# Two decode layers on one core: twelve partitions for a quarter MB of the last w2, other cuts of w1, and an earlier hand-over between two PSUM banks

## The chip, the cores and the metric

The kernel runs on one core of a Trainium2 chip. The metric is the device time of one execution in microseconds, the median of several runs. Everything is float32 and the batch is 8 rows of one token each, so the kernel reads far more than it computes with: 368.46 MB of weights and caches go from the chip's memory into the core's on-chip memory in each execution.

## What is computed

Two layers, each an attention block and then a dense block, with the same weights both times:

```python
x = x + attn(layernorm(x))       # q = x @ wq [1024 x 4096]; 32 heads of 128, 4 kv heads, 4096 cached keys
x = x + mlp(layernorm(x))        # gelu(x @ w1 [1024 x 3584] + b1) @ w2 [3584 x 1024] + b2
x = x + attn(layernorm(x))
x = x + mlp(layernorm(x))
```

`attn` takes the softmax of the scores over all cached keys and ends with `wo` [4096 x 1024].

## The kernel before, in words

All loads go into one large buffer, `arena` (L59), 128 partitions with 218 units of 1 KB in each. One unit of all partitions is 128 KB. `take` and `give` (L68, L72) mark units as used and free. All loads stand in one list, `stream`, in the order of their use (L526 to L545). `pump` (L178) is called at each `give`: as long as the first load of the list finds its units free, it is issued from the SyncE queue (SP) as one DMA over all 128 partitions. At run time SP then waits, load by load, until the engines that last read or wrote those units have finished with them.

Weights and caches lie on the partitions so that each matmul has 32 columns of weights (the batch, padded) and up to 512 columns of data. Four such matmuls, for four groups of 32 columns of TensorE, can run side by side; each writes its own 32 partitions of a PSUM bank. I call such a group a strip. A float32 matmul of the program is two matmul records in the trace, called passes here (a transpose is one).

The stages of a layer are `expand("q")` (L192), the attention over 8 batch rows (L460), `project("o")` (L288), `expand("i")` for w1 and `project("p")` for w2.

- `expand` works in two units of output columns, for w1 1792 columns each. For each unit it goes through the 8 blocks of 128 input rows (kt), at L209. After a unit its result is scaled by VectorE (DVE, L234, L237), and `hidden_unit` (L272) is put off until a later `flush`: it transposes the unit with matmuls (L246), adds b1 and computes gelu on DVE and ScalarE (ACT).
- `project` goes through the 28 blocks of 128 hidden columns (kt), each four units of w2 wide. In layer 1 the first `pairs` = 25 blocks go by 512 columns into a second PSUM bank `y2` (L327), even blocks into strips 0 and 1, odd ones into 2 and 3. Then ACT copies that bank to `scratch` (`fold`, L310) and four matmuls add the copy into the first bank `y` (`add_fold`, L313, whose matmuls have the line L295 of the helper `into`). The blocks 25 to 27 go by 256 columns straight into `y`. Half way, at block 14, `add_bias` (L298) adds b2: DVE makes four diagonals (L302), one matmul takes them into `y2` (L307), DVE makes four more in the same buffer, a second matmul takes those; then x itself is added (L350).
- The end of the kernel is the last `project`, an ACT copy of `y` into `x_row` (L358) and the output DMA (L637).

In layer 0 the weights go through a ring of four slots of 1 MB (L518). In layer 1 they are loaded in large pieces: w1 as two pieces of 56 units (L544), w2 as seven pieces of 40, 28, 20, 12, 6, 4 and 2 units (L545). I call these seven pieces w2.0 to w2.6.

In the attention, the maximum of each row of scores is spread over the partitions by a diagonal, which DVE makes (L396), and a matmul with ones (L400).

Of the kernel before, what the change touches and what calls it, by code (L numbers as in the profile page):

```python
# [39 lines left out]
AT_QZ, AT_ROW, AT_S, AT_ROW2 = 200, 208, 212, 203  # L40
AT_H = 200
Q_AT = (0, 48, 72, 32)
# [5 lines left out]
@with_exitstack  # L48
def decode_layers(ctx: ExitStack, tc: tile.TileContext, x, kc, vc, wq, wo, w1, w2, out):

# [43 lines left out]
    row_x = scratch  # L94
    r_at, dg_at, nb_at, dl_at, rl_at = 0, 2 * DH, 3 * DH, 3 * DH + HQ, 3 * DH + 2 * HQ

# [11 lines left out]

    def open_last():
        take(AT_H, 6, "last")  # L110
        nc.gpsimd.memset(place(AT_H, 5), 0.0)
        nc.vector.tensor_reduce(sel_f.rearrange("p (h m) -> p h m", h=2), ident.rearrange("p (e h m) -> p h m e", e=2, h=2), AX.X, ALU.add)
        nc.vector.tensor_scalar(nmean4.rearrange("p (j m) -> p j m", j=4), sel_x.unsqueeze(1).to_broadcast([P, 4, HQ]), -1.0 / D, None, op0=ALU.mult)
# [77 lines left out]

    def expand(name, unit, rs, finish, hooks={}, tail=(), hold=0):  # L192
        heights = [(unit // P - j + 3) // 4 * P for j in range(4)]
        for u in range(2):
            acc = big_ps()
# [76 lines left out]
    def hidden_unit(u, wide=False):  # L272
        nt = NFT // 2
        t0 = u * nt
# [12 lines left out]

    def project(name, n_k, lhs, rsum, hooks={}, bias=None, halves=False, pairs=0):  # L288
        y = big_ps()
# [25 lines left out]

        w = 32 if rsum is None else B
        g = 0
        for i, base, n_kb in loads(name):
            for c in range(n_kb):
# [3 lines left out]
                if kt < pairs:  # L323
                    if q % 2 == 0:
                        assert c + 1 < n_kb
                        j = kt % 2 * 2 + q // 2
                        nc.tensor.matmul(y2[32 * j:32 * j + 32, :], mine, arena[:, e:e + CH], start=(kt < 2), stop=(kt >= pairs - 2))  # L327
                else:
                    cut = [(q, 0, Q4)] if kt < n_k - 1 or not halves else [(2 * (q % 2) + i, q // 2 * P, P) for i in range(2)]
                    for j, a, n in cut:  # L330
                        into(j, a, n, mine, arena[:, e:e + n], stop=(kt == n_k - 1 and a + n == Q4 and (not pairs or bias is not None)))
                        e += n
                g += 1
                if c + 1 == n_kb:
# [39 lines left out]
    def scores(key, spare=False, late=False):  # L374
# [10 lines left out]
        if j == HKV - 1:  # L385
# [108 lines left out]
    def weights(name, dram, parts, kept=0):  # L494

        for u in range(dram.shape[0]):
            a = 0
            end = dram.shape[2] - (kept if u == 1 else 0)
            for i, (at, n) in enumerate(parts[u]):
                cols = min(n * KB, end - a)  # L500
                stream.append((((name, u) if dram.shape[0] > 1 else name, i), at, n, dram[u, :, a:a + cols]))
                a += cols
# [112 lines left out]
    for layer in range(2):  # L615
        pieces.update({key: at for (e, key), at in places.items() if e == layer})
        rs = layernorm(x_row, rsum)
        if layer == 0:
            expand("q0", W, rs, query_unit, {(1, "end"): keep}, hold=6)
            flush()  # L620
            last = attention(range(B), kept, after={6: park, 7: set_aside})
            set_aside_rest()
        else:
            expand("q1", W, rs, query_unit_late, {(0, 4): clear, (0, "end"): put_back_rest, (1, 3): put_back, (1, 6): open_queries_late}
                   | {(1, i): (lambda key=key: early(key)) for i, key in zip((1, 2, 4, 5), first)}, tail=(moves[1], stays))
# [6 lines left out]
        rs = layernorm(x_row, rsum, whole=layer == 1)  # L632
        expand(f"i{layer}", F // 2, rs, lambda u: hidden_unit(u, wide=layer == 1))
# [6 lines left out]
_INS = ['A_x', 'A_k_cache', 'A_v_cache', 'A_wq', 'A_wo', 'B_w1', 'B_w2']  # L640

# [17 lines left out]
def _down(w):  # L659
    return w.reshape(1, -1, P, D).transpose(0, 2, 1, 3).reshape(1, P, -1)  # L660


def _down_halves(w):
    import numpy as _np
    r = _np.array(_down(w))
    t = r[:, :, -D:].reshape(1, P, 4, 2, P)
    r[:, :, -D:] = t.transpose(0, 1, 3, 2, 4).reshape(1, P, D)
    return r


def _across(w):
    return w.reshape(NT, P, 2, -1).transpose(2, 1, 0, 3).reshape(2, P, -1)

# [4 lines left out]
    'A_v_cache': lambda a: a.reshape(B, HKV, P, -1).transpose(0, 2, 1, 3).reshape(B, P, -1),  # L678
    'A_wq': _across,
    'B_w1': _across,  # L680
    'A_wo': _down,
    'B_w2': _down_halves,
}

# [22 lines left out]
```

## Time and profile before

| | us |
|---|---|
| median of 3 runs (870.35 to 871.34) | 871.21 |
| the profiled execution, its own time | 870.82 |
| its span in the profile | 869.0 |
| PE, DVE, ACT busy in the span | 537.0, 180.3, 52.9 |

The profiled execution is 0.39 us below the median; 1.82 us of its time lie outside the span. Times in the views count from the start of the span. "DMA share" is the mean busy share of the core's 16 DMA engines, and a share a little over 1.00 comes from transfers that overlap in the records. PEclk is the granted clock of TensorE as a part of 2.4 GHz. In the timeline, a row is a run of instructions of one line, with its start, its length and their number; in brackets stands the idle time of the engine before it and what ended it.

### The profile page before, as it was taken

How to read it: one execution, taken by the hardware profiler on the slowest of the kernel's cores; microseconds unless marked ns; L12 is line 12 of the kernel's file. 1: busy time of each engine (PE TensorE's matmuls, PEld its weight loads, DVE VectorE, ACT ScalarE, POOL GpSimd, SP SyncE). 2: the span in 40 equal slices, each digit the busy share in tenths (PEclk: the TensorE clock that was granted, in tenths of full speed). 3: DMA queues.
4: the chain of work that ended last, by engine and by line, in shares of the span. 5: the costliest groups of instructions: out<-in, count | busy, mean ns of one | idle time of the engine just before them, and what ended most of it. 6: DMA issues, size and time to landing. Idle time of an engine off the chain costs nothing.

```text
span 869.0 us, 8920 instructions
## 1 busy us (share of the span) xinstructions
PE 537.0 (62%) x3932; PEld 179.6 (21%) x3932; DVE 180.3 (21%) x603; ACT 52.9 (6%) x84; POOL 3.5 (0%) x14
## 2 busy tenths in 40 slices
PE   0456574655657576866576777777564655655566
PEld 0112121211212122222232122222121211211222
DVE  0001231313122232200110033332231313120011
ACT  0100000000000011000000010000000000000100
POOL 0000000000000000000000000000000000000000
PEclk9877787777777788768977798977787777777889
DMA  9999999999999999999999999999999999999997
GB/s 393 434 435 435 429 432 432 434 432 432 434 429 432 434 419 428 412 416 418 421 420 417 408 425 438 434 434 432 432 435 431 435 434 435 432 431 436 426 422 295
DMA packets 17078, 369.06 MB, mean 425 GB/s; under 512 B 1904, under 2 KB 2064, under 8 KB 3728
## 3 DMA queue, kind: packets, MB, share of 16 engines
q1 hardware_dynamic: 16896, 368.35, 99.2%
q8 instruction: 30, 0.49, 0.2%
q10 hardware_dynamic: 144, 0.15, 0.1%
q14 instruction: 8, 0.07, 0.0%
HBM read 368.46 MB, written 0.03 MB: 424 GB/s over the span
## 4 chain that ended last, share of the span: by engine, by line
DMA 74%; PE 22%; DVE 2%; ACT 1%; issue 0%; SPq 0%; ACTq 0%; DVEq 0%
DMA arena<-in_A_k_cache_dram 26%; DMA arena<-in_A_v_cache_dram 22%; DMA arena<-in_B_w_dram 15%; DMA arena<-in_A_wq_dram 8%; PE sps L440 7%; PE sps L383 6%; DMA arena<-in_A_wo_dram 4%; PE sps L209 3%; PE sps L295 2%; PE sps L327 1%; PE sps L455 1%; PE sps L418 1%; PE sps L246 0%; ACT arena L407 0%; DVE arena L391 0%
## 5 line engine op out<-in xcount | busy, mean ns | idle before, releaser
L383 PE MATMUL sps<-arena 128*32 128x512 f32 x992 | 144.2, 720 | 119.5 <-DMA arena<-in_A_k_cache_dram 107.4
L440 PE MATMUL sps<-arena 128*32 128x512 f32 x1024 | 149.2, 722 | 9.0 <-DMA arena<-in_A_v_cache_dram 8.9
L209 PE MATMUL sps<-arena,xnT 128*32 128x512 f32 (+3 forms) x656 | 77.8, 580 | 50.4 <-DMA arena<-in_B_w_dram 26.5
L383 PEld LDWEIGHTS sps<-arena 128*32 128x32 f32 x992 | 31.5, 125 | 197.1 <-DMA arena<-in_A_k_cache_dram 99.5
L448 DVE SCALAR_TENSOR_TENSOR scratch<-sps,misc,scratch 128x128 f32<-128x128 f32 x192 | 67.4, 351 | 6.8
L295 PE MATMUL sps<-arena,oT 128*32 128x256 f32 (+1 forms) x504 | 46.3, 503 | 25.5 <-DMA arena<-in_B_w_dram 12.4
L418 PE MATMUL sps<-ident,arena 128*128 128x128 f32 x128 | 30.5, 382 | 43.5 <-ACT arena L407 31.6
L440 PEld LDWEIGHTS sps<-arena 128*32 128x32 f32 x1024 | 32.7, 129 | 83.0 <-issue 70.9
L391 DVE TENSOR_SCALAR_CACHE_REDUCE arena<-sps 128x512 f32<-128x512 f32 x32 | 22.1, 691 | 126.8 <-PE sps L383 126.8
L407 ACT ACTIVATE arena<-arena,bias 128x1024 f32<-128x1024 f32 x16 | 18.4, 1147 | 493.4 <-DVE scratch L404 493.4
L457 DVE TENSOR_TENSOR oT<-sps,scratch 128x8 f32<-128x8 f32 x64 | 11.1, 173 | 156.9 <-PE sps L455 156.9
L209 PEld LDWEIGHTS sps<-arena,xnT 128*32 128x32 f32 x656 | 22.1, 122 | 94.4 <-DMA arena<-in_A_wq_dram 36.1
L455 PEld LDWEIGHTS sps<-misc,scratch 128*128 128x128 f32 x128 | 21.7, 213 | 66.2 <-DVE scratch L448 40.9
L446 DVE TENSOR_SCALAR scratch<-sps,misc 128x128 f32<-128x128 f32 x64 | 22.0, 344 | 53.0 <-PE sps L440 53.0
L418 PEld LDWEIGHTS sps<-ident,arena 128*128 128x128 f32 x128 | 19.4, 188 | 52.1 <-ACT arena L407 35.3
L327 PE MATMUL sps<-arena,oT 128*32 128x512 f32 x120 | 17.6, 744 | 17.9 <-DMA arena<-in_A_wo_dram 17.9
L455 PE MATMUL sps<-misc,scratch 128*128 128x8 f32 x128 | 27.6, 288 | 1.3 <-DVE scratch L448 1.3
L295 PEld LDWEIGHTS sps<-arena,oT 128*32 128x32 f32 x504 | 17.2, 136 | 52.4 <-DMA arena<-in_A_wo_dram 19.8
L400 PE MATMUL sps<-scratch,misc 128*128 128x128 f32 x32 | 7.8, 326 | 19.1 <-DVE scratch L396 18.8
L423 DVE COPY arena<-sps 128x512 f32<-128x512 f32 x16 | 11.1, 692 | 38.9 <-PE sps L418 38.9
L327 PE MATMUL sps<-arena 128*32 128x512 f32 x100 | 14.4, 669 | 5.7 <-DMA arena<-in_B_w_dram 5.7
L425 PE MATMUL sps<-scratch,misc 128*128 128x32 f32 x32 | 10.0, 404 | 12.5 <-DVE arena L423 12.5
(99 smaller groups left out, 160.4 us busy)
## 6 DMA issues: line engine op xcount, KB each, us to landing
arena<-in_B_w_dram SPq DMA_DIRECT2D x26, 1024.0 KB, 8.5
arena<-in_A_wo_dram SPq DMA_DIRECT2D x15, 1024.0 KB, 8.3
arena<-in_B_w_dram SPq DMA_DIRECT2D x2, 7168.0 KB, 45.0
arena<-in_A_wq_dram SPq DMA_DIRECT2D x13, 1024.0 KB, 8.1
arena<-in_A_k_cache_dram SPq DMA_DIRECT2D x3, 4096.0 KB, 18.3
arena<-in_A_v_cache_dram SPq DMA_DIRECT2D x3, 4096.0 KB, 24.5
arena<-in_A_v_cache_dram SPq DMA_DIRECT2D x4, 2048.0 KB, 12.0
arena<-in_B_w_dram SPq DMA_DIRECT2D x1, 5120.0 KB, 39.8
```

Of the source, the lines that this page charges most:

```text
L209: nc.tensor.matmul(acc[32 * j:32 * j + 32, r * P:(r + len(ts)) * P], xnT[:, kt * B:kt * B + 32], blocks[:, ts[0] - t0:ts[-1] - t0 + 1:4], ...
L295: nc.tensor.matmul(y[32 * j:32 * j + 32, a:a + n], weights, data, start=(j not in begun), stop=stop)
L327: nc.tensor.matmul(y2[32 * j:32 * j + 32, :], mine, arena[:, e:e + CH], start=(kt < 2), stop=(kt >= pairs - 2))
L383: nc.tensor.matmul(ps[32 * g:32 * g + 32, :], q[:, c:c + 32], kt[:, g * CH:(g + 1) * CH], start=(j == 0), stop=(j == HKV - 1))
L391: nc.vector.tensor_scalar(row[:, half * CH:(half + 1) * CH], ps, SCALE, None, op0=ALU.mult, op1=ALU.max, accum_out=st["mx"][:, half:half + 1])
L407: nc.scalar.activation(row, row, AF.Exp, bias=bias, scale=1.0, accum_out=ls)
L418: nc.tensor.transpose(pp[:, t * P:(t + 1) * P], row[:, c:c + P], ident)
L423: nc.vector.tensor_copy(s[:, half], src)
L440: nc.tensor.matmul(o[32 * g:32 * g + 32, :], s[:, g], v[:, g * CH:(g + 1) * CH], start=(half == 0), stop=(half == NH - 1))
L446: nc.vector.tensor_scalar(r, o[:, 0:P], sel_t[:, 0:1], None, op0=ALU.mult)
L448: nc.vector.scalar_tensor_tensor(r, o[:, t * P:(t + 1) * P], sel_t[:, t:t + 1], r, op0=ALU.mult, op1=ALU.add)
L455: nc.tensor.matmul(po[:, 0:REP], scratch[:, a:a + DH], sel_h, start=True, stop=True)
```

## The change

Three things, each in a few lines of the diff.

1. **w2 of layer 1.** The first 512 columns of the first w2 block (128 rows of 2 KB, 256 KB) are no longer part of w2.0 to w2.6, whose sizes become 40, 28, 18, 12, 6, 4, 2 units. These 128 rows are laid out again, on 12 partitions in 11 groups (the last has 8 rows, padded to 12): 12 rows of 22 KB, 264 KB. Four DMAs load them, each with three rows: partitions m, m+4, m+8 for m = 0 to 3. They stand in the stream after w1 and ahead of w2.0. So that matmuls can use them, the weights of that block are cut into the same 11 groups: 11 small matmuls with the identity and two DVE copies (`low_weights`) at the start of the last `project`. After block 8, 11 matmuls over 12 partitions (`low_products`) add the groups into `y2`, into strips 0 and 2 in turn. The hidden values' buffer moves from unit 200 to 212 to make room.
2. **w1 in 2048 and 1536 columns** instead of twice 1792, in both layers. In layer 1 the two pieces are then 64 and 48 units.
3. **22 blocks in the second bank** instead of 25: `fold` comes after block 21, and the blocks 22 to 27 go straight into `y`.

Besides, the diagonal of the attention's maximum goes: one transpose (a single pass) of the broadcast maximum takes the place of L396 and L400. In layer 0, the last w2 block is taken by four matmuls in place of eight.

```diff
+FU = (2048, 1536)
-AT_H = 200
+AT_H = 212
+AT_LOW, AT_LH = 184, 206
+LOW = 12
+NLOW = (P + LOW - 1) // LOW
...
             take(at, n, key)
-            nc.sync.dma_start(out=arena[:, at * KB:at * KB + src.shape[1]], in_=src)
+            dst = arena[:, at * KB:at * KB + src.shape[1]]
+            if key[0] == "low":
+                dst = arena[key[1]:LOW:4, AT_LOW * KB:AT_LOW * KB + src.shape[1]]
+            nc.sync.dma_start(out=dst, in_=src)
...
+        def low_weights():
+            pt = small_ps("pt")
+            for s in range(NLOW):
+                n = min(LOW, P - s * LOW)
+                nc.tensor.matmul(pt[0:n, s * 32:(s + 1) * 32], ident[:, s * LOW:s * LOW + n], lhs[:, 0:32], start=True, stop=True)
+            for a, b, n in ((0, NLOW - 1, LOW), (NLOW - 1, NLOW, P - (NLOW - 1) * LOW)):
+                nc.vector.tensor_copy(lh[0:n, a * 32:b * 32], pt[0:n, a * 32:b * 32])
+
+        def low_products():
+            for s in range(NLOW):
+                n = min(LOW, P - s * LOW)
+                at = AT_LOW * KB + s * CH
+                into2(s % 2 * 2, lh[0:n, s * 32:(s + 1) * 32], arena[0:n, at:at + CH])
...
+        if low:
+            low_weights()
+            g = 2
...
+                if low and kt == 8:
+                    low_products()
...
-                nc.vector.tensor_scalar(scratch[:, dg_at:dg_at + P], ident, nm, None, op0=ALU.mult)
+                st["nm"] = nm
...
-        nc.tensor.matmul(pm[:, 0:P], ones, scratch[:, dg_at:dg_at + P], start=True, stop=True)
+        nc.tensor.transpose(pm[:, 0:P], st.pop("nm").to_broadcast([P, P]), ident)
...
-    weights("i0", w1, [halved(ring[0:7], 0), [(R[(7 + i) % 4], TILE) for i in range(7)]])
+    weights("i0", w1, [halved(ring[0:8], 0), ring[0:6]])
...
-    weights("i1", w1, [[(Bb, 56)], [(C, 56)]])
-    weights("p1", w2, [[(A, 40), (A + 40, 28), (A + 68, 20), (A + 88, 12), (A + 100, 6), (A + 106, 4), (A + 110, 2)]])
+    weights("i1", w1, [[(Bb, 64)], [(C, 48)]])
+    for m in range(4):
+        stream.append((("low", m), AT_LOW, 2 * NLOW if m == 0 else 0, w2_low[m:LOW:4, :]))
+    weights("p1", w2[:, CH:], [[(A, 40), (A + 40, 28), (A + 68, 18), (A + 86, 12), (A + 98, 6), (A + 104, 4), (A + 108, 2)]])
...
-        project(f"p{layer}", NFT, h_wide if layer == 1 else hT, rsum, bias=b2T, halves=True, pairs=layer * (NFT - 3))
+        project(f"p{layer}", NFT, h_wide if layer == 1 else hT, rsum, bias=b2T, halves=True, pairs=layer * (NFT - 6), low=layer == 1)
```

Two places where the order of instructions matters. The first is TensorE from the end of w1 to the end of the kernel. L327 is a w2 matmul into `y2`, L307 the bias, L295 a matmul into `y` (from `x_all` for x, from `scratch` for the fold, from `arena` for w2). Before:

```order
L327 MATMUL sps<-arena 32x512 x8
L246 MATMUL sps<-ident,scratch 128x128 x3
L246 MATMUL sps<-ident,scratch 128x64
L327 MATMUL sps<-arena 32x512 x20
L307 MATMUL sps<-scratch,misc 32x512 x2
L295 MATMUL sps<-x_all,arena 32x256 x4
L327 MATMUL sps<-arena 32x512 x22
L295 MATMUL sps<-arena 32x256 x4
L295 MATMUL sps<-scratch,arena 32x256 x4
L295 MATMUL sps<-arena 32x256 x4
L295 MATMUL sps<-arena 32x128 x8
```

With the change L338 is `low_weights`, L329 a matmul into `y2` (the 11 of `low_products` are among the 31), L316 the bias and L304 a matmul into `y`:

```order
L338 MATMUL sps<-arena,ident 12x32 x10
L338 MATMUL sps<-arena,ident 8x32
L329 MATMUL sps<-arena 32x512 x7
L255 MATMUL sps<-ident,scratch 128x128 x3
L329 MATMUL sps<-arena 32x512 x31
L316 MATMUL sps<-scratch,misc 32x512 x2
L304 MATMUL sps<-x_all,arena 32x256 x4
L329 MATMUL sps<-arena 32x512 x16
L304 MATMUL sps<-arena 32x256 x4
L304 MATMUL sps<-scratch,arena 32x256 x4
L304 MATMUL sps<-arena 32x256 x16
L304 MATMUL sps<-arena 32x128 x8
```

Ahead of the bias 28 matmuls become 38; between the bias and the fold 22 become 16; behind the fold's four there are 24 in place of 12.

The second place is SP's queue from the last `wo` on (L182 before, L191 now; 256 columns are one unit). Before:

```order
L182 DMA arena<-in_A_wo_dram 128x16384 x2
L182 DMA arena<-in_B_w_dram 128x14336 x2
L182 DMA arena<-in_B_w_dram 128x10240
L182 DMA arena<-in_B_w_dram 128x7168
L182 DMA arena<-in_B_w_dram 128x5120
```

With the change:

```order
L191 DMA arena<-in_A_wo_dram 128x16384 x2
L191 DMA arena<-in_B_w_dram 128x16384
L191 DMA arena<-in_B_w_dram 128x12288
L191 DMA arena<-in_low_dram 3x5632 x4
L191 DMA arena<-in_B_w_dram 128x10240
L191 DMA arena<-in_B_w_dram 128x7168
L191 DMA arena<-in_B_w_dram 128x4608
```

The four loads of three rows stand between w1 and w2.0, and w2.2 is 512 columns smaller.

## Rows read from the trace of the kernel before

**Rows 1.** The page: busy time by engine, and DMA in 40 slices.

```profile
PE 537.0 (62%) x3932; PEld 179.6 (21%) x3932; DVE 180.3 (21%) x603; ACT 52.9 (6%) x84; POOL 3.5 (0%) x14
...
DMA  9999999999999999999999999999999999999997
```

**Rows 2.** Stretches of the span: engines, granted clock, DMA share, GB/s.

```profile
40.00:300.00 260.00, 155.00 (x980) 49.33 (x984) 59.81 (x198) 13.36 (x20) 0.00 (x0) 0.76 1.00 432
300.00:500.00 200.00, 134.74 (x1204) 47.53 (x1196) 29.98 (x102) 14.04 (x24) 0.16 (x1) 0.79 1.01 417
500.00:700.00 200.00, 131.79 (x934) 44.29 (x930) 60.26 (x197) 12.84 (x20) 0.68 (x1) 0.82 1.01 433
700.00:858.00 158.00, 97.65 (x658) 31.30 (x662) 27.74 (x97) 8.28 (x14) 1.17 (x1) 0.78 1.00 430
...
852.00:858.00 6.00, 5.03 (x30) 1.40 (x26) 0.98 (x5) 0.00 (x0) 0.00 (x0) 0.74 0.94 401
858.00:864.00 6.00, 6.00 (x55) 2.56 (x51) 0.00 (x0) 0.25 (x1) 0.00 (x0) 1.00 0.76 311
```

**Rows 3.** The same view of the last microseconds, columns as in rows 2.

```profile
860.00:861.00 1.00, 1.00 (x15) 0.42 (x8) 0.00 (x0) 0.00 (x0) 0.00 (x0) 1.00 0.89 358
861.00:861.50 0.50, 0.50 (x11) 0.10 (x8) 0.00 (x0) 0.00 (x0) 0.00 (x0) 1.00 0.71 287
...
862.50:863.00 0.50, 0.50 (x6) 0.11 (x1) 0.00 (x0) 0.00 (x0) 0.00 (x0) 1.00 0.53 209
...
864.00:864.50 0.50, 0.21 (x5) 0.11 (x8) 0.00 (x0) 0.34 (x1) 0.00 (x0) 1.00 0.36 139
864.50:865.00 0.50, 0.50 (x12) 0.31 (x15) 0.00 (x0) 0.00 (x0) 0.00 (x0) 1.00 0.06 21
```

**Rows 4.** DMA queues: packets, MB, share of 16 engines' span.

```profile
q1 hardware_dynamic: 16896, 368.35, 99.2%
q8 instruction: 30, 0.49, 0.2%
```

**Rows 5.** Timeline of PE, from the last wo to w1's end.

```profile
797.10 7.86 PE L327 MATMUL sps<-arena,oT 128*32 128x512 f32 x56 [9.19 <-DMA arena<-in_A_wo_dram]
814.12 4.44 PE L209 MATMUL sps<-arena,xnT 128*32 128x512 f32 x24 [5.62 <-DMA arena<-in_B_w_dram]
...
818.81 4.49 PE L209 MATMUL sps<-arena,xnT 128*32 128x512 f32 x40
...
830.97 3.63 PE L209 MATMUL sps<-arena,xnT 128*32 128x512 f32 x16 [7.68 <-DMA arena<-in_B_w_dram]
```

**Rows 6.** Timeline of PE and SP: SP's last loads; PE in the last w2.

```profile
767.83 55.54 SPq L182 DMA_DIRECT2D arena<-in_B_w_dram  x9
...
843.20 1.92 PE L327 MATMUL sps<-arena 128*32 128x512 f32 x16 [2.64 <-DMA arena<-in_B_w_dram]
845.74 2.78 PE L327 MATMUL sps<-arena 128*32 128x512 f32 x24
851.62 3.62 PE L327 MATMUL sps<-arena 128*32 128x512 f32 x16 [3.10 <-DMA arena<-in_B_w_dram]
855.02 1.06 PE L307 MATMUL sps<-scratch,misc 128*32 128x512 f32 x2
858.36 5.31 PE L327 MATMUL sps<-arena 128*32 128x512 f32 x40
863.29 0.81 PE L295 MATMUL sps<-arena 128*32 128x256 f32 x8
```

**Rows 7.** The chain that ended last, its end: start, length, what.

```profile
857.05 0.51 PE sps L307
...
858.31 5.38 PE sps L327 x41
863.69 0.03 ACTq L310
863.71 0.04 issue
863.75 0.59 ACT scratch L310
864.35 0.04 issue
864.39 1.55 PE sps L295 x32
865.94 0.02 issue
865.97 0.37 ACT x_all L358
```

**Rows 8.** Groups by line, of DVE and PE, over the span.

```profile
L396 DVE TENSOR_SCALAR scratch<-ident,nm 128x128 f32<-128x128 f32 x16 | 4.7, 295 | 0.6
```

**Rows 9.** DMA issues: KB each, us to landing; then the issuing line: ns, first to last start.

```profile
arena<-in_B_w_dram SPq DMA_DIRECT2D x1, 256.0 KB, 42.2
...
L182 SPq DMA_DIRECT2D arena<-in_B_w_dram x39: 327/328/667, 389.1 to 822.9; - x39
```

More of the change, by code (lines that the diff above doesn't have):

```diff
@@ L48, in decode_layers @@
 @with_exitstack
-def decode_layers(ctx: ExitStack, tc: tile.TileContext, x, kc, vc, wq, wo, w1, w2, out):
+def decode_layers(ctx: ExitStack, tc: tile.TileContext, x, kc, vc, wq, wo, w1, w2, w2_low, out):
     nc = tc.nc
@@ L109, in open_last @@
     def open_last():
+        give(*stays)
         take(AT_H, 6, "last")
+        take(AT_LH, 2, "last")
         nc.gpsimd.memset(place(AT_H, 5), 0.0)
@@ L190, in loads, with expand @@
             i += 1
-    def expand(name, unit, rs, finish, hooks={}, tail=(), hold=0):
-        heights = [(unit // P - j + 3) // 4 * P for j in range(4)]
-        for u in range(2):
+    def expand(name, units, rs, finish, hooks={}, tail=(), hold=0):
+        for u, unit in enumerate(units):
+            heights = [(unit // P - j + 3) // 4 * P for j in range(4)]
             acc = big_ps()
@@ L286, in hidden_unit, with project @@
         nc.vector.scalar_tensor_tensor(to[:, t0 * B:t0 * B + n], g, 1.0, pre, op0=ALU.add, op1=ALU.mult)
-    def project(name, n_k, lhs, rsum, hooks={}, bias=None, halves=False, pairs=0):
+    def project(name, n_k, lhs, rsum, hooks={}, bias=None, halves=False, pairs=0, low=False):
         y = big_ps()
@@ L316, in project, with into2 @@
         w = 32 if rsum is None else B
+        begun2 = set()
+        def into2(j, weights, data, stop=False):
+            nc.tensor.matmul(y2[32 * j:32 * j + 32, :], weights, data, start=(j not in begun2), stop=stop)
+            begun2.add(j)
+        lh = place(AT_LH, 2)[0:LOW, 0:NLOW * 32]
+        def low_weights():
[11 more added lines that the diff above has]
+            for m in range(4):
+                held.pop(("low", m))
+            give(AT_LOW, 2 * NLOW)
         g = 0
+        if low:
+            low_weights()
+            g = 2
         for i, base, n_kb in loads(name):
@@ L326, in project @@
                         j = kt % 2 * 2 + q // 2
-                        nc.tensor.matmul(y2[32 * j:32 * j + 32, :], mine, arena[:, e:e + CH], start=(kt < 2), stop=(kt >= pairs - 2))
+                        into2(j, mine, arena[:, e:e + CH], stop=(kt >= pairs - 2))
                 else:
-                    cut = [(q, 0, Q4)] if kt < n_k - 1 or not halves else [(2 * (q % 2) + i, q // 2 * P, P) for i in range(2)]
+                    cut = [(q, 0, Q4)]
+                    if halves and kt == n_k - 1:
+                        cut = [(2 * (q % 2) + i, q // 2 * P, P) for i in range(2)] if pairs else []
                     for j, a, n in cut:
@@ L332, in project @@
                         e += n
+                    if not cut and q == 3:
+                        assert c >= 3
+                        last = arena[:, e + KB - D:e + KB].rearrange("p (i j n) -> p j i n", i=2, j=4)
+                        for j in range(4):
+                            into(j, 0, Q4, mine, last[:, j], stop=True)
                 g += 1
@@ L494, in weights @@
     def weights(name, dram, parts, kept=0):
-        for u in range(dram.shape[0]):
-            a = 0
-            end = dram.shape[2] - (kept if u == 1 else 0)
+        a = 0
+        ends = [dram.shape[1]] if len(parts) == 1 else [NT * (FU[0] if name[0] == "i" else W), dram.shape[1] - kept]
+        for u, end in enumerate(ends):
             for i, (at, n) in enumerate(parts[u]):
                 cols = min(n * KB, end - a)
-                stream.append((((name, u) if dram.shape[0] > 1 else name, i), at, n, dram[u, :, a:a + cols]))
+                stream.append((((name, u) if len(parts) > 1 else name, i), at, n, dram[:, a:a + cols]))
                 a += cols
@@ L543, in decode_layers @@
     weights("o1", wo, [[(C, SLOT), (A, SLOT)]])
-    weights("i1", w1, [[(Bb, 56)], [(C, 56)]])
-    weights("p1", w2, [[(A, 40), (A + 40, 28), (A + 68, 20), (A + 88, 12), (A + 100, 6), (A + 106, 4), (A + 110, 2)]])
+    weights("i1", w1, [[(Bb, 64)], [(C, 48)]])
+    for m in range(4):
+        stream.append((("low", m), AT_LOW, 2 * NLOW if m == 0 else 0, w2_low[m:LOW:4, :]))
+    weights("p1", w2[:, CH:], [[(A, 40), (A + 40, 28), (A + 68, 18), (A + 86, 12), (A + 98, 6), (A + 104, 4), (A + 108, 2)]])
     kept = set(k_keys(7)) | set(v_keys(7)) | set(k_keys(6))
@@ L618, in decode_layers @@
         if layer == 0:
-            expand("q0", W, rs, query_unit, {(1, "end"): keep}, hold=6)
+            expand("q0", (W, W), rs, query_unit, {(1, "end"): keep}, hold=6)
             flush()
@@ L665, in _down_halves, with _low, _across, laid @@
     r = _np.array(_down(w))
-    t = r[:, :, -D:].reshape(1, P, 4, 2, P)
-    r[:, :, -D:] = t.transpose(0, 1, 3, 2, 4).reshape(1, P, D)
-    return r
-def _across(w):
-    return w.reshape(NT, P, 2, -1).transpose(2, 1, 0, 3).reshape(2, P, -1)
+    t = r[:, -D:].reshape(P, 4, 2, P)
+    r[:, -D:] = t.transpose(0, 2, 1, 3).reshape(P, D)
+    return r
+def _low(w):
+    import numpy as _np
+    r = _np.zeros((NLOW * LOW, CH), _np.float32)
+    r[0:P] = w[0:P, 0:CH]
+    return r.reshape(NLOW, LOW, CH).transpose(1, 0, 2).reshape(LOW, -1)
+def _across(first):
+    def laid(w):
+        import numpy as _np
+        halves = (w[:, :first], w[:, first:])
+        return _np.concatenate([h.reshape(NT, P, -1).transpose(1, 0, 2).reshape(P, -1) for h in halves], axis=1)
+    return laid
 _LAYOUT = {
@@ L678 @@
     'A_v_cache': lambda a: a.reshape(B, HKV, P, -1).transpose(0, 2, 1, 3).reshape(B, P, -1),
-    'A_wq': _across,
-    'B_w1': _across,
+    'A_wq': _across(W),
+    'B_w1': _across(FU[0]),
     'A_wo': _down,
     'B_w2': _down_halves,
+    'low': _low,
 }
@@ L695 @@
     for name in _INS:
-        own = [name] if name != 'A_x' else [name, 'B_b1', 'B_b2']
-        a = _np.ascontiguousarray(_LAYOUT[name](*(_np.asarray(inputs[n]) for n in own)))
+        a = _np.ascontiguousarray(_LAYOUT[name](*(_np.asarray(inputs[n]) for n in _OF.get(name, [name]))))
         arrays[f"in_{name}_dram"] = a
```

15 lines of the change are left out of this document (8 added, 7 removed).

## The prediction

> **What bounds the kernel now.** I read the page first. TensorE is busy 62% of the span and no other engine more than 21%, while the DMA line shows 9 in 39 of its 40 slices [rows 1]. The stretches say the same more finely: from 40 to 858 us the share is 1.00 or 1.01 in each of the four long stretches, with 417 to 433 GB/s [rows 2]. So the 16 DMA engines never rest, and whatever shortens a chain of matmuls or of DVE work in these 858 us moves idle time of those engines about and no end. Only two things can move the end: how many bytes the busiest DMA engine has to carry, and what comes behind its last byte.
>
> The last microseconds show how unequal the 16 are [rows 3]. The share is 0.89 from 860 to 861, 0.71 in the next half microsecond, 0.53 by 862.75, 0.36 by 864.25 and 0.06 behind 864.5. A share of 0.71 is 11.4 engines at work, 0.36 is 5.8. So some four or five engines have nothing left at about 861.2, and about six work until about 864.6, 3.4 us longer. The time that all 16 could save if the rest were shared out evenly is the idle share summed up to 864.6: about 1.8 us. One cause stands in the queue rows: 30 loads of code of 16 KB [rows 4]. Their 0.2% of 16 x 869 us is 27.8 us, 0.93 us each, and each stays with the engine that did it. Which engine did which, no view names.
>
> Behind the last byte, the chain has ACT's copy for the fold at 863.75, then 32 matmuls from 864.39 to 865.94, ACT's copy of the result, and the output [rows 7]. The last load, 256 KB, is issued at 822.9 and lands 42.2 us later, at 865.1 [rows 9]. The matmuls of the chain were under way by then; TensorE and the last byte end nearly together, and TensorE is a little later.
>
> **The change, part by part.**
>
> *The quarter MB.* Of every load over 128 partitions each DMA engine carries a sixteenth. 433 GB/s at a share of about 1.00 [rows 2] is 27.1 GB/s for an engine. Taking 256 KB out of w2.2 takes 16 KB from each engine: 0.60 us. The four new loads bring 264 KB. The trace has no load of so few rows, so I bound it: spread over all 16, it costs 0.62 us on each and the step is worth nothing; on one engine alone, 9.98 us. I take three engines, a row each, since each row is one run of bytes to one partition: 88 KB, 3.33 us on each of the three. Net: thirteen engines end 0.60 us earlier, three end 2.73 us later than they would have.
>
> What that is worth hangs on the lead of these three. With a lead of 3.3 us or more, as four or five engines have [rows 3], they still end first, and the last byte lands 0.60 us earlier, at 864.5. This is what I take. With a smaller lead they are last themselves.
>
> The Trainium skill ("DMA: Bandwidth & Descriptors", section on why a DMA increments its semaphore by 16) says that a load's engine count is the largest number up to 16 that divides its slowest dimension, and that they are the lowest-numbered ones; by that it is three engines, always the same. The page's rules for authors say to use all 16, since a small outer dimension confines a DMA to few engines; were all 16 equally late, by that rule the end would come 2.73 us later. Rows 3 show that they are not equally late here, and no row shows which are early.
>
> The new loads' place costs nothing on SP: SP issues its last nine loads from 767.83 on and is done with them at 823.4 [rows 6], while w2.0 is waited for by TensorE until 843.20. That is some 20 us of cover; without it each of the four issues would cost about 0.33 us (328 ns) [rows 9].
>
> *w1 as 2048 and 1536 columns.* In layer 1 the first piece now needs one more tile of the last values consumed, eight matmuls, about 1 us later than 767.83; the wo load ahead of it lands only at 797.1 [rows 5], so 29 us cover it. The piece is 8 MB in place of 7 and lands 2.4 us later than 814.1, at 816.5; the two together still land at 831.0. TensorE takes 9 us for a piece (4.44 + 4.49 [rows 5]), done by 826, ahead of 831. The second piece is smaller and its work ends earlier, which leaves room for `low_weights` ahead of 843.20, where TensorE waits 2.64 us. Cost: nothing. In layer 0 there are 24 matmuls fewer and the last block has four for eight, where the share is 1.01 (300 to 500) [rows 2]: nothing. Cover gone, it would be a gain, under 24 x 2 x 0.3 us side by side by four, some 4 us.
>
> *The maximum's diagonal.* 16 DVE instructions of 295 ns go, 4.7 us in all [rows 8], and as many passes; all beside full DMA: nothing.
>
> *TensorE in the last w2.* Block by block, with 24 passes of 512 columns in 2.78 us, 0.116 us each with four strips side by side [rows 6]. `low_products` has 11 matmuls, 22 passes, in two strips: twice that, 0.232 us each, 5.1 us. No row shows matmuls over 12 partitions; a bound below is four strips' rate, 2.6 us, one above is one strip at a time, 0.46 us, 10.2 us. I take 5.1 as the strips 0 and 2 alternate. Before, TensorE finished w2.0 at 848.52 (845.74 + 2.78) and waited 3.10 us. Now it works on to 853.6. Then it is 2.0 us late for w2.1, but it has not idled: the first 16 passes of w2.1 took 3.62 us before, against 1.86 at the later rate (the granted clock was 0.74 from 852 to 858, a mixture of 1.2 and 2.4 GHz, and 1.00, which is 2.4 GHz, from 858 on [rows 2]), and now there are 14, 1.6 us. The bias comes at 855.2, as before (855.02). From it to the end of w2.2 there are 32 passes in both kernels, so that falls at about 861.4, where before TensorE turned to w2.3.
>
> Here the hand-over moves. Before, w2.3's passes came first, to 863.69, then the fold's copy (0.59), then 32 passes (1.55) to 865.94 [rows 7]. Now the copy starts at 861.5, while block 22 goes into `y`: eight passes of 256 columns, 0.43 us at half the price of 512. The fold's four at 862.1 to 862.5, blocks 23 and 24 to 863.4, w2.4 to 864.0, w2.5 to 864.5. Then w2.6, landed at 864.5: eight passes of 128 columns and their drain, some 0.5 us: 865.0 instead of 865.94. That is 0.9 us earlier. If `low_products` costs 1 us more than I take, TensorE ends as before. So the sum lies between 0 and 0.9 earlier; I take 0.6, since both the last byte and TensorE must come early for the whole of it.
>
> **Sum.** 865.94 - 0.6 in the profiled execution, whose 869.0 of span and 1.82 around it otherwise stay: 870.2 of its own time. It was 0.39 below the median of 871.21, so I forecast 871.2 - 0.6 = 870.6. That is 0.07%; a measurement of this kernel can tell about 0.2%, 1.7 us, from no change.
>
> **The rivals.**
>
> *The three engines become the last.* If one of them is among the six that work until 864.6, its last byte comes 2.73 us later, the last load lands at 867.8 instead of 865.1, and with 0.5 us of matmuls behind it TensorE ends at 868.3: 2.4 us later, 873.6, slower. It decides as soon as a lead is under 3.3 us; it costs from a lead of about 2.4 on, because TensorE's gain pays for the first part. For it: eleven engines are still at work behind 861, and few rows are needed for a bad place. Against it: the leading engines are a block of four or five, and code loads that come again and again to the same engines would leave the same neighbours free; that the lowest three are among the free ones is my judgement, no row says it. In the middle, one engine with a lead near 1.7 us: landing 1.0 us later, 871.9.
>
> *TensorE late.* If the 22 passes run one strip at a time, or at 1.2 GHz, they take 10.2 us, all 5.1 more are behind the wait of 3.10 already used, and less 0.9 that is 4.2 later: 875.4. For it: two bias passes in one strip took 1.06 us [rows 6]. Against it: the strips alternate.
>
> *The load is not three engines' work.* All on one: 9.98 - 0.60 less a lead of 3.4 is 6.0 later, 877. On all 16: no change of the landing, 870.9.
>
> **Chances.** Forecast 0.68 (mostly within 0.6 of 870.6); the middle case 0.08; three engines last 0.12; TensorE late 0.07; one engine 0.02; something that makes it faster by more than this sum, such as code loads that fall otherwise, 0.03. Faster by over 0.2% (under 869.5): that last 0.03 and the lower edge of the forecast, 0.05. Slower: 0.12 + 0.07 + 0.02 and a little of the middle case, 0.22. Within: 0.73. The range from 869.6 to 873.0 holds the forecast, the middle case and the part of the first rival where the engine is only partly last.
>
> **What would show it.** In the profile after, the staircase of the DMA share at the end should begin about 0.6 us earlier at its foot, with no early plateau of 0.71 left: three more engines at work until about 863.9. If instead three engines work on alone (a share near 0.19 for over 1 us), the first rival holds. TensorE should have no wait ahead of w2.1; the 31 matmuls' rows between 843 and 855 should be without a gap, at a granted clock of 1.00; ACT's fold copy should stand near 861.5 and no wait for it ahead of the last matmuls. The 40 to 858 stretch should keep its share of 1.00. A wait of TensorE for the fold at the end, or w2.1 begun behind 856, would make the second part wrong.

## The result, and the profile after

| | before | with the change |
|---|---|---|
| median of 5 runs, us | 871.21 (870.35 to 871.46) | 874.64 (873.74 to 875.20) |
| profiled execution, its span | 870.82, 869.0 | 873.74, 872.0 |
| end of the last matmul in the span | 865.94 [rows 7] | 868.66 |

The ratio, of the means, is 1.0042, with a 95% interval from 1.0031 to 1.0053: slower by 3.4 us in the median, outside the forecast's range of 869.6 to 873.0. The profiled execution of the change is the fastest of its five, so what its trace shows is rather less than the loss of the median.

The queue of SP and TensorE's end of the timeline come first. SP's rows answer to the first of [rows 6], TensorE's to the others. L338 is `low_weights`, L316 the bias, L319 (on ACT) the copy for the fold.

```profile
767.94 17.97 SPq L191 DMA_DIRECT2D arena<-in_B_w_dram  x2
787.42 2.92 SPq L191 DMA_DIRECT2D arena<-in_low_dram  x4
804.29 28.25 SPq L191 DMA_DIRECT2D arena<-in_B_w_dram  x7
...
830.77 2.79 PE L218 MATMUL sps<-arena,xnT 128*32 128x384 f32 x16 [5.26 <-DMA arena<-in_B_w_dram]
...
839.53 0.81 PE L338 MATMUL sps<-arena,ident 128*12 128x32 f32 x22
842.89 2.97 PE L329 MATMUL sps<-arena 128*32 128x512 f32 x14 [2.56 <-DMA arena<-in_B_w_dram]
845.79 0.90 PE L255 MATMUL sps<-ident,scratch 128*128 128x128 f32 x3
846.62 11.72 PE L329 MATMUL sps<-arena 128*32 128x512 f32 x62
858.17 1.02 PE L316 MATMUL sps<-scratch,misc 128*32 128x512 f32 x2
861.47 3.20 PE L329 MATMUL sps<-arena 128*32 128x512 f32 x27
866.27 2.35 PE L304 MATMUL sps<-arena 128*32 128x256 f32 x48
```

The wait ahead of w2.0 is what it was (2.56 for 2.64), and the second piece of w1 begins where it did. From 842.89 on TensorE has no wait for data at all, neither ahead of w2.1 nor at the end. But the bias stands at 858.17, where before it stood at 855.02. The row of 62 passes holds the next 16 passes of w2.0, the 22 passes over 12 partitions (848.65 to about 853.8 by their single records), the last 10 passes of w2.0 and the first 14 of w2.1. For in the kernel the products come when eight blocks (0 to 7) are done, ahead of block 8 and not behind it, so they do not stand at the end of w2.0.

What stretched these rows is seen in stretches of TensorE alone: length, busy time with the number of passes, granted clock, DMA share, GB/s.

```profile
840.00:842.00 2.00, 0.34 (x12) 1.00 0.87 375
842.00:844.00 2.00, 1.11 (x11) 0.90 1.00 430
844.00:846.00 2.00, 2.00 (x11) 0.50 1.00 430
846.00:848.00 2.00, 2.00 (x15) 0.74 1.00 431
848.00:850.00 2.00, 2.00 (x16) 1.00 1.01 432
850.00:852.00 2.00, 2.00 (x12) 1.00 0.92 390
852.00:854.00 2.00, 2.00 (x12) 0.96 1.01 426
854.00:856.00 2.00, 2.00 (x12) 0.50 0.94 390
856.00:858.00 2.00, 2.00 (x16) 0.68 0.99 417
```

The granted clock is 0.50, which is 1.2 GHz, twice: from 843.6 to 847.0 and from 853.9 to 857.3 by its records. In the kernel before, the last w2 has one such stretch, 851.7 to 855.1, and it begins as TensorE's wait of 3.10 us for w2.1 ends, at 851.62 [rows 6]. Here TensorE is busy for the whole of each 2 us around the second fall. A pass of 512 columns is 0.59 us long by the single records of 852 to 853 and 1.06 us by those of 854 to 856.

The transfers did not come later, but earlier. The same view with all engines (PE, PEld, DVE, ACT, POOL) and the last microseconds, as in [rows 3]:

```profile
861.00:861.50 0.50, 0.50 (x9) 0.36 (x9) 0.00 (x0) 0.00 (x0) 0.00 (x0) 1.00 0.86 352
...
863.50:864.00 0.50, 0.50 (x8) 0.21 (x4) 0.00 (x0) 0.00 (x0) 0.00 (x0) 1.00 0.10 37
864.00:864.50 0.50, 0.50 (x10) 0.24 (x5) 0.00 (x0) 0.00 (x0) 0.00 (x0) 1.00 0.00 0
```

A share of 0.86 stands where 0.71 stood, and at 864.0 all is loaded, where before 0.36 of the engines worked on to 864.5. By the records of its landing, the last load is there at 864.32 (865.15 before, 864.5 predicted). The chain that ended last (start, length, what) now runs through TensorE and no longer near the last byte:

```profile
846.69 11.65 PE sps L329 x62
858.34 0.86 PE sps L316 x2
...
861.42 3.70 PE sps L329 x28
...
865.18 0.59 ACT scratch L319
865.77 0.04 issue
865.82 2.85 PE sps L304 x56
```

So TensorE ends some 4.7 us behind the last byte. The theory from here on: the loss is TensorE, and of it the granted clock. The rivals were the three engines, the hand-over, w1, and the length of the products itself. Theory letters in the expectations are told in each of them.

### The profile page after: what moved, and what is told of

Same layout as the page of the kernel before. It is cut to its first block, busy times and chain, and to the rows that moved or that the text cites. A ratio compares the mean times of both kernels' runs of the same rounds, so it can differ in the third digit from the quotient of the medians.

```text
span 872.0 us, 8877 instructions
## 1 busy us (share of the span) xinstructions
PE 545.4 (63%) x3912; PEld 172.7 (20%) x3912; DVE 175.2 (20%) x585; ACT 52.9 (6%) x84; POOL 3.5 (0%) x14
## 4 chain that ended last, share of the span: by engine, by line
DMA 72%; PE 24%; DVE 2%; ACT 1%; issue 0%; SPq 0%; ACTq 0%; DVEq 0%
DMA arena<-in_A_k_cache_dram 27%; DMA arena<-in_A_v_cache_dram 16%; DMA arena<-in_B_w_dram 11%; DMA arena<-in_A_wq_dram 9%; DMA arena<-in_A_wo_dram 8%; PE sps L486 7%; PE sps L429 7%; PE sps L329 3%; PE sps L218 3%; PE sps L304 2%; PE sps L501 1%; PE sps L464 1%; ACT arena L453 1%; DVE arena L437 1%; DVE scratch L494 0%
## 5 line engine op out<-in xcount | busy, mean ns | idle before, releaser
L429 PE MATMUL sps<-arena 128*32 128x512 f32 x992 | 146.1, 729 | 117.8 <-DMA arena<-in_A_k_cache_dram 105.6
L486 PE MATMUL sps<-arena 128*32 128x512 f32 x1024 | 152.0, 734 | 16.5 <-DMA arena<-in_A_v_cache_dram 16.5
L218 PE MATMUL sps<-arena,xnT 128*32 128x512 f32 (+3 forms) x608 | 81.0, 661 | 41.5 <-DMA arena<-in_B_w_dram 22.7
L304 PE MATMUL sps<-arena,oT 128*32 128x256 f32 x496 | 45.9, 501 | 25.0 <-DMA arena<-in_A_wo_dram 13.1
L464 PE MATMUL sps<-ident,arena 128*128 128x128 f32 x128 | 26.8, 344 | 43.6 <-ACT arena L453 31.7
L218 PEld LDWEIGHTS sps<-arena,xnT 128*32 128x32 f32 x608 | 17.8, 126 | 91.8 <-DMA arena<-in_A_wq_dram 31.4
L329 PE MATMUL sps<-arena,oT 128*32 128x512 f32 x120 | 18.3, 769 | 19.0 <-DMA arena<-in_A_wo_dram 19.0
L464 PEld LDWEIGHTS sps<-ident,arena 128*128 128x128 f32 x128 | 16.8, 167 | 51.5 <-ACT arena L453 35.5
L304 PEld LDWEIGHTS sps<-arena,oT 128*32 128x32 f32 x496 | 16.2, 133 | 52.9 <-DMA arena<-in_A_wo_dram 20.8
L329 PE MATMUL sps<-arena 128*32 128x512 f32 (+2 forms) x108 | 19.0, 701 | 2.6 <-DMA arena<-in_B_w_dram 2.6
L471 PE MATMUL sps<-scratch,misc 128*128 128x32 f32 x32 | 10.2, 412 | 12.5 <-DVE arena L469 12.5
L157 PE MATMUL sps<-nmean,rsum 128*128 128x64 f32 x8 | 2.0, 337 | 25.3 <-DVE rsum L604 23.6
```

The lines of the kernel that those rows point to most:

```text
L218: nc.tensor.matmul(acc[32 * j:32 * j + 32, r * P:(r + len(ts)) * P], xnT[:, kt * B:kt * B + 32], blocks[:, ts[0] - t0:ts[-1] - t0 + 1:4], ...
L304: nc.tensor.matmul(y[32 * j:32 * j + 32, a:a + n], weights, data, start=(j not in begun), stop=stop)
L329: nc.tensor.matmul(y2[32 * j:32 * j + 32, :], weights, data, start=(j not in begun2), stop=stop)
L429: nc.tensor.matmul(ps[32 * g:32 * g + 32, :], q[:, c:c + 32], kt[:, g * CH:(g + 1) * CH], start=(j == 0), stop=(j == HKV - 1))
L464: nc.tensor.transpose(pp[:, t * P:(t + 1) * P], row[:, c:c + P], ident)
L486: nc.tensor.matmul(o[32 * g:32 * g + 32, :], s[:, g], v[:, g * CH:(g + 1) * CH], start=(half == 0), stop=(half == NH - 1))
```

## The experiments

In all of them the time before is that of the runs beside them: 870.80 us (23 runs) for the first four, 870.85 (15) for the second profile of the products moved ahead and for both edits at once, 870.94 (35) for the other four. A time is the median; a ratio is of the means, with its 95% interval.

**Ten of the eleven products left out.** The loads, `low_weights` and all else stay.

```diff
-                into2(s % 2 * 2, lh[0:n, s * 32:(s + 1) * 32], arena[0:n, at:at + CH])
+                if s == 0:
+                    into2(0, lh[0:n, 0:32], arena[0:n, at:at + CH])
```

> The change with its four loads of three rows and its 11 small weight matmuls, but with only the first of the 11 products over 12 partitions (120 of the 128 rows of that quarter MB are left out of the result). Theory, TensorE late: the 22 passes from 848.65 to 853.8 are what put TensorE behind the loads. Without 20 of them TensorE ends its first w2 piece near 849, waits for w2.1, and the end comes from the last byte, which in the change is about 0.8 us earlier than before: 870.0 to 871.0 us. Rival, three engines last: the loads are all there, so the time stays at 874.6. Rival, the earlier hand-over or the cut of w1 costs: 873 or more.

Measured: 869.91 us (869.88 to 871.00, 11 runs), ratio 0.9990 [0.9982, 0.9999]. The chain that ended last is a transfer again:

```profile
832.11 31.99 DMA arena<-in_B_w_dram
864.10 0.04 issue
864.14 1.12 PE sps L304 x18
```

The granted clock fell once, 842.8 to 846.3, and stayed at 1.00 behind it. With every load of the change in place the kernel ends with the last byte, so by themselves neither the three engines nor w1 nor the hand-over costs the 3.4 us. It takes the products, with what hangs on them: 4.7 us for 20 passes.

**No quarter MB apart.** w2 goes in seven whole pieces as before, with `low` off; w1 in 2048 and 1536 and 22 blocks stay.

```diff
-    for m in range(4):
-        stream.append((("low", m), AT_LOW, 2 * NLOW if m == 0 else 0, w2_low[m:LOW:4, :]))
-    weights("p1", w2[:, CH:], [[(A, 40), (A + 40, 28), (A + 68, 18), (A + 86, 12), (A + 98, 6), (A + 104, 4), (A + 108, 2)]])
+    weights("p1", w2, [[(A, 40), (A + 40, 28), (A + 68, 20), (A + 88, 12), (A + 100, 6), (A + 106, 4), (A + 110, 2)]])
```

> The change without the quarter MB: w2 whole, in pieces of 40, 28, 20, 12, 6, 4, 2 units; w1 in 2048 and 1536 columns, 22 blocks in the second bank. Theory, TensorE late: no extra passes, the last byte as before the change, the fold's copy no longer in the way: 870.5 to 871.2 us, equal to before or 0.5 better. Rival, the cut of w1 (by another granted clock in the last w2) or the hand-over costs: 872.5 to 874.6.

Measured: 870.39 us (870.25 to 870.64, 11 runs), 0.9995 [0.9987, 1.0004]: no change against before, and all of the loss gone. The granted clock fell once here too, within a wait of 4.55 us ahead of w2.0 (838.47 to 843.02), from 841.4 to 848.3; TensorE still had 0.84 us to wait ahead of w2.1 and 0.92 ahead of w2.3.

**33 partitions, 11 loads.** Four products in place of 11.

```diff
-LOW = 12
+LOW = 33
...
-                dst = arena[key[1]:LOW:4, AT_LOW * KB:AT_LOW * KB + src.shape[1]]
+                dst = arena[key[1]:LOW:LOW // 3, AT_LOW * KB:AT_LOW * KB + src.shape[1]]
```

> The change with the quarter MB on 33 partitions in place of 12: 11 loads of three rows of 8 KB, the same bytes, and 4 products over 33 partitions in place of 11 over 12. Theory, TensorE late: 8 passes in two strips, about 1.8 us in place of 5.2, so TensorE is 3.4 us less late and the last byte decides: 870.0 to 871.2 us. Rival, three engines last: the three engines carry the same bytes, so 874.6 or more.

Measured: 877.56 us (877.16 to 877.90, 5 runs), 1.0075 [1.0063, 1.0087]. A miss, and of a new kind: fewer products, but SP was held up. Its timeline:

```profile
787.09 47.47 SPq L191 DMA_DIRECT2D arena<-in_low_dram  x11
834.66 3.44 SPq L191 DMA_DIRECT2D arena<-in_B_w_dram  x7
849.28 3.63 PE L329 MATMUL sps<-arena 128*32 128x512 f32 x14 [8.80 <-DMA arena<-in_B_w_dram]
```

Issuing w2.0 waited behind the eleven loads until 834.66 (804.29 in the change), and the 16 engines ran dry:

```profile
815.00:830.00 15.00, 8.91 (x66) 0.84 0.87 352
830.00:836.00 6.00, 4.12 (x24) 0.50 0.38 115
```

What SP waited for between 786 and 836 (us in total, times, longest):

```profile
SPq L191 <- DMA arena<-in_B_w_dram: 33.7, 2, 18.7
SPq L191 <- DMA arena<-in_A_wo_dram: 6.2, 1, 6.2
```

SP's single records say why it waits for landings of other weights. The program marks its loads with eight semaphores in turn, and an issue waits until the load eight places ahead of it, which had the same semaphore, has landed. The first five of the eleven were out at 790.7; the sixth went at 796.87, when the last wo piece had landed, the seventh at 816.21 behind w1's first piece, the eighth at 831.86 behind its second. The run tells nothing of the products, but where the cover that the prediction named for the four issues ends: at the number of loads under way.

**25 blocks in the second bank, as before.** `NFT - 6` becomes `NFT - 3` in the call of `project`.

> The change with 25 blocks in the second bank, as before the change. Theory, TensorE late: TensorE has as many passes in all and now waits for the fold's copy at the end, about 0.3 to 0.8 us more than the change: 874.9 to 875.5 us. Rival, the hand-over at 22 is what costs: near 872 us.

Measured: 875.00 us (874.23 to 878.91, 6 runs), 1.0052 [1.0038, 1.0066], against 874.64 for the change. The hand-over does not cause the loss. What it gains when TensorE ends last, the two spreads do not tell. The profiled execution, the slowest, has the clock at 0.5 almost throughout from 852 to 862, with TensorE busy:

```profile
848.00:852.00 4.00, 4.00 (x26) 0.88 0.96 410
852.00:862.00 10.00, 10.00 (x34) 0.52 0.93 385
```

**The same products over 128 partitions.** Nothing is left out: the buffer of the cut weights is zeroed on all partitions, and the 11 matmuls take all 128 rows of weights and data, so that 116 of them add zero. Passes, columns and strips are the same.

```diff
-        lh = place(AT_LH, 2)[0:LOW, 0:NLOW * 32]
+        lh = place(AT_LH, 2)[:, 0:NLOW * 32]
...
+            nc.gpsimd.memset(lh, 0.0)
...
-                into2(s % 2 * 2, lh[0:n, s * 32:(s + 1) * 32], arena[0:n, at:at + CH])
+                into2(s % 2 * 2, lh[:, s * 32:(s + 1) * 32], arena[:, at:at + CH])
```

> The change with the same 11 products, but each as a matmul over all 128 partitions: the weights of the other 116 partitions are zero, so the passes, their columns and their strips are the same and only the number of rows differs. Theory A: the products over 12 partitions are what the granted clock falls after (1.00 from 847.0, 0.5 from 853.9 to 857.3 in the change, with TensorE busy all the while). With 128 rows there is no such fall, TensorE is about 1.7 us earlier: 872.3 to 873.3 us. Rival B: the fall comes with the place of the work and not with the rows: 874 to 875.2 us, and the granted clock falls again behind the products.

Measured: 871.84 us (870.27 to 872.95, 11 runs), 1.0011 [1.0002, 1.0019]: 2.8 us less than the change, and below what either theory had given it. The stretches, columns as above:

```profile
844.00:846.00 2.00, 2.00 (x10) 0.50 0.96 411
846.00:848.00 2.00, 2.00 (x18) 0.84 1.03 441
...
852.00:854.00 2.00, 2.00 (x18) 1.00 1.02 436
854.00:856.00 2.00, 2.00 (x18) 1.00 0.98 401
```

The first fall is there (843.2 to 846.6), the second is not, and the bias comes at 856.30 instead of 858.17. That is 1.87 us, and the two profiled executions differ by as much (873.74 and 871.87). A stretch of 3.4 us at half the rate costs an engine that is never idle in it 1.7 of them. The products themselves start every 0.43 us in both, two passes side by side. The medians differ by 2.80; the 0.9 us beyond the two traces are not explained by them.

**The 12-partition products ahead of w2.0.** `low_products()` is called right behind `low_weights()` instead of after block 8, so that it uses the wait there.

> The change with its 11 products directly behind the 11 weight matmuls, ahead of the first w2 piece, in place of behind block 8. Theory, TensorE late: TensorE waits 2.56 us there for w2.0 (842.89) and the kernel without the quarter MB waits 4.55; some 2 us of the 5.2 are then free, and the rest uses the wait ahead of w2.1 (0.84). The last byte decides nearly: 870.0 to 871.3 us. Rival (the products' 5.2 us cost the same wherever they stand, or the granted clock falls behind them by more): 873 to 874.6 us.

Measured: 872.85 us (869.89 to 873.33, 12 runs), 1.0010 [0.9999, 1.0020]. The executions lie at two values, five from 869.9 to 870.4 and seven from 872.7 to 873.3. The profiled one is of 870.42. A second execution was profiled:

> The variant with the products over 12 partitions ahead of the w2 units, looked at once more, since its executions lay at two values (870.3 and 873.1) and the trace shows one at 870.4. If this execution is one at 873, theory A expects a second stretch at granted clock 0.5 late in the last w2, of about 3.4 us, and a bias about 1.7 us later or more; theory B (a late byte) expects the same clock and a DMA share that ends later. If it is one at 870.4, the trace repeats: one stretch at 0.5 from 844 to 851.

It took 873.36 us. The two show one long fall each, and no second one, so the form expected was wrong, but the clock was what differed. Over the whole span, too, the five executions near 870 had a granted clock of 0.788 to 0.793, the seven near 873 one of 0.782 to 0.788. First the execution of 870.42, cut at the clock's edges:

```profile
836.00:844.40 8.40, 7.83 (x75) 1.00 1.01 435
844.40:851.20 6.80, 6.80 (x27) 0.50 0.96 413
851.20:865.00 13.80, 12.51 (x140) 1.00 0.78 325
```

And that of 873.36:

```profile
836.00:843.50 7.50, 6.93 (x78) 0.96 1.00 430
843.50:853.70 10.20, 10.20 (x33) 0.50 0.99 425
853.70:869.00 15.30, 13.22 (x148) 1.00 0.54 222
```

The bias went from 854.84 to 857.75, and the end of TensorE behind the last byte. Of these 2.91 us, 1.7 are the price of 3.4 us more at 0.50. The other 1.22 were there when the products began, at 840.92 instead of 839.70: in w1's second piece the clock was at 0.50 until 836.6 and not only until 834.2. The same program, with TensorE busy through both stretches: why the one lasts 6.8 and the other 10.2 us, no view says.

**15 partitions, 5 loads, 9 products, ahead of w2.0.** `LOW = 15`, and the call moved as above.

> The quarter MB on 15 partitions, five loads of three rows, nine products (18 passes, about 3.9 us in place of 5.2), ahead of the first w2 piece. Theory, TensorE late: TensorE has the products done some 1.3 us earlier than with 12 partitions and the last byte decides: 869.8 to 870.6 us, if the SP queue is not held up as it was with eleven loads (there SP issued the last of them at 834 and w2.0 landed 6 us late, at 849.2). Rival, SP held up by more loads in flight: above 872 us.

Measured: 871.53 us (870.48 to 872.93, 11 runs), 1.0005 [0.9997, 1.0014], about a microsecond more than expected. SP is not held up (3.62 us for the five issues). The granted clock is 0.5 from 841.9 to 852.1, so fewer passes and three more rows did not keep it up.

**No quarter MB and 25 blocks.** What remains of the change is w1, the maximum and layer 0's last block.

> Without the quarter MB and with 25 blocks in the second bank: only w1's cut, the attention's maximum and layer 0's last block are left of the change. Against the kernel with 22 blocks and no quarter MB (870.39) this prices the hand-over alone. Theory: the fold's copy stands again between w2.3 and the last matmuls, TensorE ends about 0.4 us later: 870.6 to 871.2 us, the time of before. Rival, the hand-over is worth nothing once the last byte decides: 870.4 us.

Measured: 870.29 us (870.12 to 870.51, 11 runs), 0.9991 [0.9983, 1.0000]; with 22 blocks it was 870.39. The chain here ends with the fold's copy (863.38, 0.59 us) and 32 passes (864.02 to 865.62), and with 22 blocks with a transfer and 18 passes (864.37 to 865.48). So the hand-over does take the copy out of the end, but is worth nothing that these times tell.

**128 rows and ahead of w2.0, both at once.** The two edits above.

> Both edits at once: the 11 products read 128 partitions (zero weights on those that hold no data) and run right behind the transposed weights, ahead of the w2 units. With 128 rows alone the granted clock was 1.00 from 846.6 on and TensorE ended 1.9 us earlier than in the change, but still 1.9 us behind the transfers; moved ahead alone, executions lay at 870.3 and at 873. Theory A (the clock falls behind the passes over 12 partitions, and the 5 us that the products take after 848 are the rest of the loss): clock 1.00 from 849 on at the latest, bias by 855, the end set by the last byte, 869.8 to 870.6 in nearly every execution, below the kernel before by up to 1 us. Theory B (the clock falls whatever the rows, by chance): executions at 870 and at 873 as with 12 rows, median 870.5 to 873.

Measured: 869.92 us (869.76 to 870.67, 11 runs), 0.9986 [0.9977, 0.9995]: faster than the kernel before by about 1 us, less than the 0.2% named in the prediction, but with an interval that ends below 1, and 4.7 us faster than the change, with nothing left out. One row of TensorE's stretches is enough:

```profile
836.00:866.00 30.00, 25.59 (x253) 1.00 0.87 368
```

No fall at all from 836.2 to the end. The chain ends with the last byte, even in the profiled execution, which is the slowest of the eleven:

```profile
831.87 32.57 DMA arena<-in_B_w_dram
864.44 0.04 issue
864.48 1.12 PE sps L304 x18
```

The runs side by side; the stretches at 0.5 are from 838 us to the end, in the profiled execution:

| passes of `low_products` | granted clock 0.5 | bias | median us |
|---|---|---|---|
| none (kernel before) | 851.7-855.1 | 855.02 | 870.8 to 871.2 |
| none (no quarter MB, 22 blocks) | 841.4-848.3 | 853.18 | 870.39 |
| 2 over 12 rows (ten products left out) | 842.8-846.3 | 852.73 | 869.91 |
| 22 over 12 rows (the change) | 843.6-847.0, 853.9-857.3 | 858.17 | 874.64 |
| 22 over 12 rows, 25 blocks | 842.1-849.0, 852.4-862.6 | 862.93 | 875.00 |
| 22 over 128 rows | 843.2-846.6 | 856.30 | 871.84 |
| 22 over 12 rows, early | 844.4-851.2 or 843.5-853.7 | 854.84 or 857.75 | 872.85 |
| 18 over 15 rows, early | 841.9-852.1 | 855.94 | 871.53 |
| 22 over 128 rows, early | none | 853.07 | 869.92 |

## Why the prediction was wrong

**What bounds the kernel: right, and it still bounds it once TensorE is out of the way.** In the profiles of the variants at 869.91, 869.92 and 870.39 us the chain ends with the last byte.

**The quarter MB: right, a little too large.** The lead was there. By the records of landings, each of the four loads landed on three engines, where a load over 128 partitions lands on sixteen, and they took 0.85 us one behind the other, 826.88 to 829.60. Of w1's second piece, the load before them, seven engines were done by 826.76 and the last at 830.73, so three early ones took the rows. In the change the last load landed 0.83 us earlier than before; the share had fallen to 0.10 by 863.5 and to 0 by 864.0, and no three engines worked on alone. The sign of no early plateau near 0.71 did not hold in each run: with 128 rows early the share is 0.71 to 0.73 from 861.0 to 862.5. With TensorE out of the way the quarter MB is worth 870.39 - 869.92 = 0.47 us by the medians, against 0.60 predicted, though the intervals of the two overlap. The Trainium skill ("DMA: Bandwidth & Descriptors", section on why a DMA increments its semaphore by 16) gives the lowest-numbered engines to such loads; the records agree with three engines and show no numbers. The first rival falls.

**The loads on SP: right, with less cover than it seemed.** The four issues took 2.92 us, 0.73 each where I had 0.33, and cost nothing that shows. What bounds the cover is the turn of the eight semaphores: it already held w2.3's issue until w1 had landed, 830.79 in place of 821.62, which was still in time. With eleven loads the issues took 47.47 us and the kernel lost 6.8.

**w1, the maximum, layer 0: right where the last byte decides.** The second piece began at 830.77 (831.0 predicted); with these parts alone the time is 870.29. Whether w1's new cut shares in the loss once TensorE ends last is open, as the next but one paragraph shows.

**`low_products`: right.** 5.1 us predicted, about 5.2 measured, at 1.00, in two strips side by side.

**The step that failed is the clock in "TensorE in the last w2".** I wrote that TensorE, late for w2.1, "has not idled", that therefore w2.1's first 14 passes take 1.6 us, and that the bias comes at 855.2. It came at 858.17, 2.97 later. The sign of no wait ahead of w2.1 came true, that of a granted clock of 1.00 from 843 to 855 did not. I had read the fall in the kernel before as the price of an idle wait that the change removes. The clock fell all the same, at 853.9, behind the passes over 12 partitions; with 128 rows in the same passes it did not, and the bias came 1.87 us sooner. The other 1.1 us go with the first fall, 843.6 to 847.0, which I had not in the sum: w2.0's first 14 passes took 2.97 us, where at the rate of before (1.92 for 16 [rows 6]) they take 1.7. So at 848.65, where my sum had all of w2.0 done (848.52), 10 of its 40 passes were still to come, 1.1 us of work. That fall is there with 128 rows, with two products and with none, so the 12-row passes do not cause it. It goes, together with the idle 2.56 us, when 128-row passes fill the wait ahead of w2.0. In the profile of the kernel before, the wait there was as long (2.64) and no fall followed; every variant has w1's new cut, and none has the products with the old one, so what this cut has to do with the first fall was not tested.

**From the bias to the fold: short by 0.7 us.** 855.2 to 861.5 is 6.3 predicted, 858.17 to 865.18 is 7.0 measured. The fold waits for all 28 passes of the chain's 3.70 us row, among which TensorE also takes block 22's eight. From the fold's copy to the end it is 3.48 (865.18 to 868.66), against 3.5.

So 865.0 + 2.97 + 0.7 = 868.7, the measured end. The hand-over worked as told, but on a TensorE that was late.

**The rival that came true in its time is "TensorE late", 875.4 with a chance of 0.07; measured 874.64.** Its mechanism was half right: not serial strips, nor the products at 1.2 GHz, but the passes of w2 around them at 1.2 GHz. That the time came so near is luck. The rows of before had the price: TensorE's end in the sum lay within 1 us of the last byte, and one stretch at half the rate costs 1.7. A term of which one fall more or less decides deserved more than 0.07.

## What to carry to other kernels

When a change fills TensorE's idle time with work of another shape, forecast TensorE's granted clock anew, and allow for one more stretch at half the rate, instead of taking the old rows without the idle time. Matmuls over few partitions were the costly ones here; the same matmuls over all partitions, with zero weights for what does not belong, took as long, and no fall followed them. Put extra work into a wait that exists already: the same eleven products cost 4.7 us behind the first eight blocks over 12 rows, and ahead of w2.0 over 128 rows nothing that shows.

## What the runs showed of the hardware

The granted clock fell while TensorE was busy without a gap. In the pair that differs only in rows (early, 12 or 128), 22 passes over 12 rows began at 839.70 and 840.92, and before they were over the clock fell to 0.50, for 6.8 and 10.2 us; with those over 128 rows it did not fall. The times agree: 873.74 us is the fastest of the change's runs, 872.95 the slowest with 128 rows at the same place. The clock itself is seen in one execution of each variant, and in two of the early one. The Trainium skill ("TensorE: Matmul & The Clock Gate", Part 1) ties the lower level to an idle engine; the rows of 853.9 to 857.3 differ from that, as no idle time stands ahead of them from 842.89 on. Busy time in the profile does not by itself tell whether the clock stays up. How many rows are enough was not tried beyond 12, 15 and 128 (the run with 33 says nothing of it), and why equal executions fall for 6.8 or 10.2 us stays open. So does whether the part of the change without the quarter MB is faster than before by the 0.4 to 0.7 us of its medians: the intervals reach 1.0000 and 1.0004.

A load of three rows landed on three engines and took 0.85 us for its 66 KB on a core whose 16 engines were all at work. With eleven loads of three rows ahead of a large one, SP's queue stood still for tens of microseconds and the DMA share fell to 0.38; with four or five it did not fall. What SP waited for is the program's turn of eight semaphores, as its records show; of a limit of the queue itself they show nothing.
